# Reordering the start of a Fourier-mixing and feed-forward kernel: a weight piece behind the input, one fold by products, an earlier second stage two

## The chip, the cores and the metric

The kernel runs on one core of a Trainium2 chip. The metric is the device time of one execution in microseconds (us). Three executions of the kernel before took 1935.2, 1939.07 and 1940.8 us; the median is 1939.07. A core has five instruction streams that run side by side and wait for each other through semaphores: PE (matrix products; loads of its weights are listed as PEld), DVE (vector), ACT (activations and copies), POOL (general purpose) and SP (here only issuing transfers). Transfers are issued by SP, ACT or POOL and carried out by 16 DMA engines.

## The reference

The input x has shape (8, 3008, 256). It goes through a Fourier transform along the sequence and one along the feature axis, of which only the real part is kept. The result, as 24064 rows of 256, goes through a feed-forward layer whose activation is h * relu6(h + 3) / 6:

```python
X = np.fft.fft(x, axis=1)
X = np.fft.fft(X, axis=2)
x = X.real.astype(np.float32).reshape(B * S, D)
h = x @ w_in                      # (256, 2048)
g = h * np.clip(h + 3.0, 0.0, 6.0) / 6.0
out = (g @ w_out).astype(np.float32)   # (2048, 256)
```

The two weights arrive as 64-bit floats and are turned into 32-bit floats on the chip.

## The kernel before, in words

**Transform.** The length 3008 is split into 47 x 64. Stage one is a product with a 47-point table (`F`), stage two a product with a 64-point table (`T`). Between the stages the spectrum changes its layout through DRAM: SP and ACT store it (`zd`, line 361, later rest at line 1102), SP reads it back as `g` (line 428). The transform along the features is folded into the first weight (`fold_w_in`: PE products with the table `C`, a copy to `W1`, then SP moves one row of W1 into `WN`, line 819). The eight sequences are worked on in four pairs. The first pair is special: its first sequence (`halves[0]`) is loaded in four pieces by eight indirect transfers, two for each piece (`load_half`, line 174), so that the feed-forward can start before the second sequence is there.

**Folding x.** Each piece is added to its mirror image, first along the features (lines 215 and 216). For pieces in `FULL` a second pass builds sums and differences in a tile `y` (lines 224 to 233), and stage one needs four wide products (lines 328, 331). For the others this second pass is left out: one small add (line 219), and PE makes up for it with four times as many products, with shorter or equal rows, that read the near and the far half separately (line 344). The pieces come in the order `ORDER` = 3, 0, 1, 2. The last one (`SPLIT`) is done in two halves (lines 204, 339, 344).

**Weights.** Sixteen pieces of 512 KB come as 64-bit numbers (`load_w`, lines 727 and 731, issued by POOL). For each: ACT takes the exponent's two halves out of the top bits (`exponent_a`, line 747), PE adds them (`exponent_b`, line 761), ACT turns the sum into a power of two (`exponent_c`, line 764), DVE makes the fraction (`mantissa`, lines 772 and 773), and DVE multiplies the two (`join`, line 781 for W_in, 787 for W_out). Pieces 0 and 1 are the first of W_in, 2 and 3 the first of W_out. Pieces 4 to 9 are issued behind a small POOL copy (`see`, line 881) that waits until `g` has landed.

**Feed-forward.** A chunk is 256 columns; a step is a chunk and a group of 2 x 128 hidden features: products u and v (line 537), then s, u, v, gates on DVE (lines 546 to 586) with a relu on ACT (583), then products with the second weight into `acc` (610, 630). There are 384 steps. In the first eight (`first_steps` and `second_steps` in turn) the remaining weight pieces are made between them.

**What sets the order.** Each engine runs its instructions in the order in which the program issues them; the order is written out by hand (a manual schedule). Tiles come from pools with a fixed number of buffers; a new tile waits until the buffer's last reader is done. Two pools matter here: `ps_d`, one PSUM bank, which takes piece 1's exponent (`own=True`), every filler written without a bank of its own, and, once `starting[0]` is False, the results of stage two; and `ps_h`, three banks for u and v. `beside(p)` puts transfers and other side work at given steps (`put(t, f, ...)`). `keep_awake(n)` is filler: n products of ones with zeros, whose result nobody reads (line 831).

Of the kernel before, what the change touches and what calls it, by code (L numbers as in the profile page):

```python
# [58 lines left out]
def kernel(  # L59
# [76 lines left out]


    ORDER = [NM - 1] + list(range(NM - 1))
    FULL = (ORDER[0], ORDER[2])
    SPLIT = ORDER[NM - 1:]  # L140

    def x_tile(pool=xpool, tag="x"):
# [46 lines left out]
    def load_half(hb, m):  # L189
        start = hb.b * N1 * N2 * D  # L190
        gather(hb.x[m], NP * NXC + m, P, start + D)
        gather(hb.xr[m], m, P, start)
# [526 lines left out]
    def load_w(j):  # L719
        kind, n, i = PIECES[j]  # L720

        pool, tag, bufs = (wpool, "st", 2) if j in STRAIGHT else (spool, "t", None) if j in (2, 3) else (xpool, "x", None)
        st = pool.tile([P, 2 * WB], I32, tag=tag, bufs=bufs, name="st")
        o = st[:].bitcast(moe_w_in.dtype)
        if kind == "in":
            cs = slice(in_column(n, i), in_column(n, i) + WB // 2)
            nc.gpsimd.dma_start(out=o.rearrange("p (c j) -> p c j", c=2),
                                in_=moe_w_in[:, cs].rearrange("(c p) f -> p c f", p=P))
        else:
            r = (2 * n + i * NF) * P  # L730
            nc.gpsimd.dma_start(out=o.rearrange("p (c j) -> p c j", c=2),
                                in_=moe_w_out[r:r + 2 * P, :].rearrange("(c p) d -> p c d", p=P))
        raw[j] = st
# [6 lines left out]

    def exponent_a(j):
        top = raw[j][:].bitcast(I16).rearrange("p (n four) -> p n four", four=4)[:, :, 3]
        for i in range(2):
            low = PM[j % len(PM)][:, i].bitcast(U8).rearrange("p (n two) -> p n two", two=2)[:, :, 0]
            nc.scalar.activation(low, top, AF.Identity, bias=bias[:, i:i + 1], scale=(1 - 2 * i) / 16.0)

# [17 lines left out]
    def mantissa(j):  # L766
        st = raw[j]
        hi = st[:].rearrange("p (n two) -> p n two", two=2)[:, :, 1]
        lo = st[:].bitcast(U32).rearrange("p (n two) -> p n two", two=2)[:, :, 0]
        top = wpool.tile([P, WB], I32, tag="top", bufs=3, name="top")  # L770
        frac = top[:].bitcast(F32)
        nc.vector.tensor_scalar(top[:], hi, 0xFFFFF, 0x100000, op0=AL.bitwise_and, op1=AL.bitwise_or)
        nc.vector.scalar_tensor_tensor(frac, lo, 2.0 ** -32, top[:], op0=AL.mult, op1=AL.add)
        fracs[j] = frac
# [47 lines left out]
    def load_t(gr, ks=slice(0, 2 * KK), queue=nc.sync):  # L822
        for b in range(2):
            queue.dma_start(out=T[b * N2:(b + 1) * N2, b, gr, :, ks], in_=c_stage2[:, gr, :, ks])


    def keep_awake(n, ps=None):
        if ps is None:
            ps = ps_d.tile([P, 2 * TB], F32, tag="d", name="awake")
        for i in range(n):  # L830
            nc.tensor.matmul(ps[:], ones[:], Z[:], start=True, stop=True)  # L831
# [50 lines left out]

    for j in range(2):
        load_w(j)
    nc.gpsimd.affine_select(E[:, 0], ones[:], pattern=[[-1, P]], compare_op=AL.is_equal, fill=0.0, base=0,
                            channel_multiplier=1)
    nc.scalar.mul(E[:, 1], E[:, 0], -1.0)
    for k, m in enumerate(ORDER):  # L890
        load_half(hb, m)
    nc.gpsimd.dma_start(out=C[:], in_=c_dim.rearrange("(h p) d -> p h d", p=P))
    load_t(0, queue=nc.gpsimd)
    for j in range(2, 4):
        load_w(j)
    for j in range(2):
        exponent_a(j)
        mantissa(j)
    exponent_b(0)
    keep_awake(2)  # L900
    exponent_b(1, own=True)
    nc.scalar.copy(zero_slot(hb), first_slot[PB:PB + N1, 0:D])
    exponent_c(0)
    exponent_c(1)
    clear_table(1)
    keep_awake(2, bank([P, 2 * TB], "awake"))
    for k, m in enumerate(ORDER):
        if m in SPLIT:
            for j in range(2):
                fold_columns(hb, m, j, nc.vector)  # L910
            join(0)
        for part in range(2) if m not in SPLIT else ():
            fold_half(hb, m, part, nc.vector)
        stage1_early(hb, m)
    later[:] = later[4:6] + later[0:4] + later[6:8]
    load_g_half(hb, 0)

    seen = wpool.tile([P, 1], F32, tag="seen", name="seen")
    see(hb.g[0][:, 0, 0:1])
    for j in range(4, 10):  # L920
        load_w(j)
    take_half(halves[1], ORDER[0], cpool, "c")
    load_half(halves[1], ORDER[0])

    join(1)
    fold_w_in(0)
    fold_w_in(1)
    mantissa(2)
    exponent_a(2)
    exponent_b(2)  # L930
# [5 lines left out]
    keep_awake(2)  # L936
    join(2)

    stage2_half(hb, 0)
    spread_by_pe(hb, bank([P, TB], "ps3")[:])  # L940
    tail(3)
    starting[0] = False
    spare = [ps_a.tile([P, 2, WB // 2], F32, tag="acc", name="spare") for h in range(2)]

# [4 lines left out]
    def beside(p):  # L949
        ahead, behind = {}, {}  # L950

        def put(t, f, *a, at=ahead):
            at.setdefault(t, []).append((f, a))

        cur = pairs[p]

        if p == 0:
            for gr in range(1, NG):
                put(gr + 1, load_t, gr)
            put(1, load_g_half, halves[0], 1)  # L960
            put(5, spread_half, halves[0], 1)
            put(NF - 1, close_w)
            for i, t in enumerate((3, 5, 7, 8)):
                put(t, mix_w_out, i)
            for gr in range(2, NSG):
                put(8 * gr - 10, load_g_half, halves[0], gr)
                put(8 * gr - 5, stage2_half, halves[0], gr)
                put(8 * gr - 4, spread_half, halves[0], gr)

            hb = halves[1]  # L970
            put(1, load_zero, zero_slot(hb), hb, nc.sync)
            for k, m in enumerate(ORDER):
                if k > 0:
                    put((5, 8, 11)[k - 1], take_half, hb, m)
                    put((5, 8, 11)[k - 1], load_half, hb, m)
                for part in range(2):
                    put((4, 6, 11, 14)[k] + part, fold_half, hb, m, part, nc.gpsimd)
                put((8, 10, 15, 18)[k], stage1_quarters, hb, m, at=behind)
            for gr in range(NSG):
                put(8 * gr + 23, load_g_half, hb, gr)  # L980
                put(8 * gr + 27 - (gr == 0), stage2_half, hb, gr)
                put(8 * gr + 28 - (gr == 0), spread_half, hb, gr)

        def s2(t, pr, gr):
            for i in range(2):
                put(t + 3 + 4 * i, stage2, pr, gr, i)
            put(t + 8, spread, pr, gr)

        for gr in range(1 if p > 0 else NSG, NG):
            if gr > 1:  # L990
                put(NST * (gr - 2) + 12, load_g, cur, gr)
            s2(NST * (gr - 1), cur, gr)
        if p + 1 < NP:
            nx = pairs[p + 1]
            for c in range(NXC):
                t = 9 * c if p > 0 else 24 + 6 * c
                put(t, load_x, nx, c)
                put(t + 3, fold, nx, c, 0, nc.gpsimd)
                put(t + 5, fold, nx, c, 1, nc.gpsimd)
                put(t + 8, stage1, nx, c, at=behind)  # L1000
            put(NST * (NG - 1) - 2, load_g, nx, 0)
            put(NST * (NG - 1) + 8, load_g, nx, 1)
            s2(NST * (NG - 1), nx, 0)
        return ahead, behind
# [14 lines left out]
    uv = mlp1_products(*chunk(0))  # L1019
    activate(*chunk(0), *uv)  # L1020

    head(4)
    head(5)
    uv = mlp1_products(*chunk(1), between=lambda: keep_awake(3))

# [30 lines left out]
    def second_steps(s):  # L1058
        j = 2 * s + 4
        if j - 2 < len(PIECES):  # L1060
            if s == 1:
                see(WN[:, NF + 2:NF + 3])
            head_b(j)
            join(j)
            head_b(j + 1)
            if s == 1:
                mlp2_first(*chunk(s), halves=(0,))
                exponent_b(j + 1)
            exponent_c(j + 1)
            if j + 2 < len(PIECES):  # L1070
                head(j + 2)
            join(j + 1)
            if j + 3 < len(PIECES):
                exponent_a(j + 3)
                if s > 1:
                    head_b(j + 3)
            if s > 1:
                mlp2_first(*chunk(s), halves=(0,))
            if s == 3:
                stage2_half(halves[0], 1)  # L1080
            mlp1(*chunk(s + 1))
            if s == 1:
                head_b(j + 3)
            return
        mlp1(*chunk(s + 1))
        combine(*chunk(s + 1))
        mlp2_first(*chunk(s), halves=(0,))
        mlp1(*chunk(s + 2))
        mlp2_first(*chunk(s), halves=(1,))
# [117 lines left out]
```

## Time and profile before

| what | us |
|---|---|
| median of three executions | 1939.07 |
| the profiled execution | 1934.84 |
| its span, first to last instruction | 1933.1 |
| PE busy | 1917.7 |
| POOL busy | 1442.3 |
| DVE busy | 1426.8 |
| ACT busy | 679.5 |
| first x piece complete, DVE starts to fold | 11.68 |
| DVE starts on the last x piece | 20.02 |
| first fold of W_in on PE | 22.75 |
| read of `g` issued | 26.88 |
| first stage two on PE | 29.83 |
| first products u | 31.63 |
| stage two of group 1 on PE | 63.45 |

The table by stage gives PE's busy time for a stretch, the timeline the start and length of each instruction, and the chain of waits follows the work that ended last back from instruction to instruction. Times in the lower rows are starts, in us from the first instruction. A busy PE is not PE at its peak: fillers count as busy.

### The profile page before, as it was taken

The numbers are of one execution on the slowest core, as the hardware profiler recorded it, in microseconds if no ns is written. First come the engines' busy times: TensorE is split into PE (matmuls) and PEld (weight loads), VectorE is DVE, ScalarE is ACT, GpSimd is POOL, SyncE is SP. The second block draws the span as 40 slices with busy tenths as digits, with TensorE's granted clock in tenths as the row PEclk, the third lists the DMA queues.
The fourth block names the chain that finished last, engine by engine and source line by source line (L and its number), as shares of the span: only waits on it lengthen the run. The fifth ranks groups of instructions, "written<-read, shape, count | busy, mean of one in ns | idle before, by whom it ended". The sixth has DMA issues, their size and how long they took to land.

```text
span 1933.1 us, 28199 instructions
## 1 busy us (share of the span) xinstructions
PE 1917.7 (99%) x9360; PEld 1652.9 (86%) x9360; DVE 1426.8 (74%) x2761; ACT 679.5 (35%) x1164; POOL 1442.3 (75%) x1650
## 2 busy tenths in 40 slices
PE   9999999999999999999999999999999999999997
PEld 5688888888988888888898888888899888888887
DVE  6867776777777777777787777777778777777777
ACT  6533333333333333333333333333333333333332
POOL 4597888896688778787678787878676667666664
PEclk9999999999999999999999999999999999999999
DMA  8432232211112222121111221221110101101000
GB/s 273 129 88 50 57 86 67 63 44 39 31 36 71 57 52 55 45 56 36 27 38 50 51 55 44 54 55 46 36 28 20 28 17 29 33 12 28 21 18 20
DMA packets 154344, 98.77 MB, mean 51 GB/s; under 512 B 121877, under 2 KB 135806, under 8 KB 154198
## 3 DMA queue, kind: packets, MB, share of 16 engines
q1 hardware_dynamic: 142130, 57.45, 12.2%
q0 software_dynamic: 11360, 39.30, 7.0%
q8 instruction: 73, 1.20, 0.3%
q14 instruction: 73, 0.60, 0.1%
q10 hardware_dynamic: 708, 0.23, 0.1%
HBM read 59.61 MB, written 37.32 MB: 50 GB/s over the span
## 4 chain that ended last, share of the span: by engine, by line
PE 95%; DVE 3%; ACT 1%; DMA 0%; issue 0%; POOL 0%; DVEq 0%; ACTq 0%; POOLq 0%
PE acc L630 56%; PE v L537 16%; PE u L537 16%; PE ps L486 2%; PE ps L279 1%; PE acc L610 1%; DVE a L586 1%; DVE s L546 1%; ACT t L583 0%; DVE o L691 0%; PE spare L813 0%; DMA xt<-in_x_dram,IX 0%; PE ps L447 0%; DVE u L567 0%; PE awake L831 0%
## 5 line engine op out<-in xcount | busy, mean ns | idle before, releaser
L600 POOL TENSOR_TENSOR c<-a 128x512 f32<-128x512 f32 (+1 forms) x375 | 469.1, 1251 | 359.8 <-PE acc L630 298.1
L630 PE MATMUL acc<-c,G 128*128 128x256 f32 (+1 forms) x3008 | 697.2, 375 | 0.0
L583 ACT ACTIVATE t<-u,half 128x512 f32<-128x512 f32 (+1 forms) x384 | 260.6, 679 | 1144.1 <-DVE u L556 1064.4
L630 PEld LDWEIGHTS acc<-c,G 128*128 128x128 f32 x3008 | 565.2, 190 | 71.6 <-POOL c L600 0.4
L546 DVE SCALAR_TENSOR_TENSOR s<-qn,WN,u 128x256 f32<-128x256 f32 (+1 forms) x768 | 330.5, 472 | 338.7 <-PE u L537 338.2
L630 PE MATMUL acc<-a,G 128*128 128x256 f32 (+1 forms) x2256 | 541.6, 375 | 0.0
L630 PEld LDWEIGHTS acc<-a,G 128*128 128x128 f32 x2256 | 421.0, 189 | 73.6 <-issue 20.2
L537 PE MATMUL v<-q,W 127*128 127x256 f32 (+1 forms) x1536 | 389.3, 375 | 1.0 <-DVE a L586 1.0
L537 PE MATMUL u<-q,W 128*128 128x256 f32 (+1 forms) x1536 | 388.0, 375 | 0.2 <-ACT q L450 0.2
L586 DVE SCALAR_TENSOR_TENSOR a<-t,u 128x512 f32<-128x512 f32 (+2 forms) x448 | 264.1, 602 | 101.4 <-ACT t L583 95.6
L537 PEld LDWEIGHTS v<-q,W 127*128 127x128 f32 x1536 | 288.0, 190 | 42.1 <-DVE a L586 2.0
L537 PEld LDWEIGHTS u<-q,W 128*128 128x128 f32 x1536 | 285.8, 190 | 36.9 <-issue 1.9
L600 POOL TENSOR_TENSOR c<-a,c 128x256 f32<-128x256 f32 (+1 forms) x375 | 268.5, 716 | 29.4
L600 POOL TENSOR_TENSOR c<-c,a 128x256 f32<-128x256 f32 (+1 forms) x375 | 268.4, 716 | 29.4
L556 DVE TENSOR_TENSOR u<-s,v 128x512 f32<-128x512 f32 x352 | 245.0, 696 | 38.1 <-DVE s L546 1.8
L586 DVE SCALAR_TENSOR_TENSOR a<-t,v 128x512 f32<-128x512 f32 (+1 forms) x480 | 263.7, 566 | 0.1
L583 ACT ACTIVATE t<-v,half 128x512 f32<-128x512 f32 (+1 forms) x384 | 260.5, 679 | 0.2 <-PE acc L630 0.2
L558 DVE TENSOR_TENSOR v<-v,s 128x512 f32<-128x512 f32 x352 | 243.9, 693 | 0.0
L600 POOL TENSOR_TENSOR r<-w,e 128x256 f32<-128x256 f32 (+1 forms) x92 | 88.7, 984 | 3.6
L640 ACT ACTIVATE e<-acc 128x512 f32<-128x512 f32 (+2 forms) x184 | 83.4, 544 | 0.0
L691 DVE STREAM_TRANSPOSE o<-r 128x256 f32<-128x256 f32 (+1 forms) x192 | 72.6, 415 | 0.2
L600 POOL TENSOR_TENSOR w<-w,e 128x512 f32<-128x512 f32 (+1 forms) x46 | 57.5, 1250 | 3.6
(133 smaller groups left out, 777.0 us busy)
## 6 DMA issues: line engine op xcount, KB each, us to landing
out_dram<-o SPq DMA_DIRECT2D x747, 32.0 KB
g<-zd SPq DMA_DIRECT2D x42, 256.0 KB
zd<-z SPq DMA_DIRECT2D x48, 192.0 KB
xt<-in_x_dram POOLq DMA_DIRECT2D x21, 256.0 KB, 3.7
st<-in_moe_w_in_dram POOLq DMA_DIRECT2D x8, 512.0 KB, 6.7
st<-in_moe_w_out_dram POOLq DMA_DIRECT2D x8, 512.0 KB, 8.4
qn<-qd SPq DMA_DIRECT2D x16, 256.0 KB
xt<-in_x_dram POOLq DMA_DIRECT2D x17, 192.0 KB, 4.1
```

The lines of the kernel that those rows point to most:

```text
L279: nc.tensor.matmul(ps[b][h * PB:(h + 1) * PB, 0:n], F[rows(b), 0:PB], y[rows(b), 2 * h:2 * h + n], start=True, stop=not last, skip_group_c ...
L486: nc.tensor.matmul(ps[:, blk, u * P:n].rearrange("p (b k) -> p b k", b=2), g[:, kk, blk * (P + 1):blk * (P + 1) + P], T[:, :, gr, blk, kk, ...
L537: nc.tensor.matmul(ps[:, i, 0:nq], W1[r, blk, f * P:(f + 1) * P], q[r, blk, of:of + nq], start=True, stop=True)
L546: nc.vector.scalar_tensor_tensor(s[:, i, 0:nq], qn[:, of:of + nq], WN[:, f:f + 1], u[:, i, 0:nq], op0=AL.mult, op1=AL.add)
L556: nc.vector.tensor_tensor(u[:], s[:], v[:], op=AL.add)
L558: nc.vector.tensor_tensor(v[:], v[:], s[:], op=AL.subtract)
L583: nc.scalar.activation(t, h, AF.Relu, bias=half[:], scale=scale)
L586: nc.vector.scalar_tensor_tensor(dst, t, 1.0, h, op0=AL.min, op1=AL.mult)
L600: (eng or nc.gpsimd).tensor_tensor(out, in0, in1, op=AL.add)
L630: nc.tensor.matmul(ch.acc[i // 2][:, i % 2, 0:ch.n], G[:, i, fc, :], mv, start=(fc == 0 and i % 2 == 0), stop=(fc == NF - 1), skip_group_c ...
L640: nc.scalar.mul(ch.e[:, k:i + 1, 0:ch.n], ch.acc[i // 2][:, 0:i + 1 - k, 0:ch.n], 1.0 / WS)
L691: nc.vector.transpose(o[:, 0:n // DH, h], ch.r[:, m, h, 0:n].rearrange("p (j i) -> p j i", i=DH))
```

## The change

- `FULL` shrinks from pieces 3 and 1 to piece 3 alone. Piece 1, the third to come, is folded along the features only and goes through the short products.
- Weight piece 1 is loaded behind the eight loads of x instead of ahead of them, and then C; pieces 2 and 3 come ahead of T(0) instead of behind it. Piece 1's exponents and mantissa move behind the first stage: the first of its two exponent halves on ACT after the third piece of x (`k == NM - 2`), the rest after the loads issued behind `see`. Its join stands behind the first `fold_w_in`, followed by one filler.
- Ahead of x, two fillers, piece 1's exponent and two fillers become five fillers in one bank.
- `g` of group 1 is read right behind `g` of group 0 (before: at step 1), and `see` looks at it. T of group 1 is loaded on SP behind the second `fold_w_in` (before: at step 2). The other T loads come one step earlier, the spread of group 1's last row at step 2 instead of 5.
- `tail(3)` comes ahead of the first stage two. Stage two of group 1 moves from step 3 to between the first chunk step's activation and the second's products; between the latter's u and v there is one filler instead of three.

```diff
-    FULL = (ORDER[0], ORDER[2])
+    FULL = ORDER[:1]
...
-    def exponent_a(j):
+    def exponent_a(j, signs=range(2)):
         top = raw[j][:].bitcast(I16).rearrange("p (n four) -> p n four", four=4)[:, :, 3]
-        for i in range(2):
+        for i in signs:
...
-    for j in range(2):
-        load_w(j)
+    load_w(0)
...
         load_half(hb, m)
+    load_w(1)
     nc.gpsimd.dma_start(out=C[:], in_=c_dim.rearrange("(h p) d -> p h d", p=P))
-    load_t(0, queue=nc.gpsimd)
     for j in range(2, 4):
         load_w(j)
-    for j in range(2):
-        exponent_a(j)
-        mantissa(j)
+    load_t(0, queue=nc.gpsimd)
+    exponent_a(0)
+    mantissa(0)
     exponent_b(0)
-    keep_awake(2)
-    exponent_b(1, own=True)
     nc.scalar.copy(zero_slot(hb), first_slot[PB:PB + N1, 0:D])
     exponent_c(0)
-    exponent_c(1)
     clear_table(1)
-    keep_awake(2, bank([P, 2 * TB], "awake"))
+    keep_awake(5, bank([P, 2 * TB], "awake"))
...
         stage1_early(hb, m)
+        if k == NM - 2:
+            exponent_a(1, (0,))
     later[:] = later[4:6] + later[0:4] + later[6:8]
     load_g_half(hb, 0)
+    load_g_half(hb, 1)
...
-    see(hb.g[0][:, 0, 0:1])
+    see(hb.g[1][:, 0, 0:1])
...
+    mantissa(1)
+    exponent_a(1, (1,))
+    exponent_b(1, own=True)
+    exponent_c(1)
+    fold_w_in(0)
     join(1)
-    fold_w_in(0)
+    keep_awake(1)
     fold_w_in(1)
+    load_t(1)
     mantissa(2)
...
+    tail(3)
     stage2_half(hb, 0)
     spread_by_pe(hb, bank([P, TB], "ps3")[:])
-    tail(3)
     starting[0] = False
...
-            for gr in range(1, NG):
-                put(gr + 1, load_t, gr)
-            put(1, load_g_half, halves[0], 1)
-            put(5, spread_half, halves[0], 1)
+            for gr in range(2, NG):
+                put(gr, load_t, gr)
+            put(2, spread_half, halves[0], 1)
...
     activate(*chunk(0), *uv)
 
+    stage2_half(halves[0], 1)
     head(4)
     head(5)
-    uv = mlp1_products(*chunk(1), between=lambda: keep_awake(3))
+    uv = mlp1_products(*chunk(1), between=lambda: keep_awake(1))
...
-            if s == 3:
-                stage2_half(halves[0], 1)
```

## The prediction

> **What bounds the kernel now.** I read the page first: busy shares and chain.
>
> ```profile
> PE 1917.7 (99%) x9360; PEld 1652.9 (86%) x9360; DVE 1426.8 (74%) x2761; ACT 679.5 (35%) x1164; POOL 1442.3 (75%) x1650
> ...
> PE 95%; DVE 3%; ACT 1%; DMA 0%; issue 0%; POOL 0%; DVEq 0%; ACTq 0%; POOLq 0%
> ```
>
> PE ends the span. A table by stage has it busy 399.8 of every 400 us from 400 to 1600 us, and the edits lie ahead of 90 us. So a microsecond won or lost there on the path moves the end by as much; the main part will not change. Next, the chain of waits of the first 40 us (start, length, what):
>
> ```profile
> 5.02 6.56 DMA xt<-in_x_dram,IX
> ...
> 17.19 1.80 PE ps L344 x30
> ...
> 19.94 0.87 PE ps L328 x6
> ...
> 21.90 0.93 PE ps L344 x32
> 22.82 3.65 PE wps L813 x16
> 26.47 0.43 PE ex L761 x2
> 26.91 0.86 PE awake L831 x2
> 27.76 0.43 PE ex L761 x2
> 28.20 1.72 PE awake L831 x4
> 29.91 1.06 PE ps L447 x8
> ...
> 34.49 2.58 PE awake L831 x6
> 37.07 0.86 PE v L537 x4
> 37.93 1.72 PE acc L610 x4
> ```
>
> Input until 11.6, folds and first stage until 22.8, then the trip of the spectrum through DRAM, which PE covers with 7.09 us of weight folding and fillers until stage two at 29.91. The timeline shows that trip:
>
> ```profile
> 23.68 0.69 ACTq L361 DMA_DIRECT2D zd<-z  x1
> ...
> 26.88 0.41 SPq L428 DMA_DIRECT2D g<-zd  x1
> ...
> 29.75 0.18 POOL L881 COPY seen<-g 128x1 f32<-128x1 f32 x1 [12.90 <-DMA g<-zd]
> ...
> 30.25 1.42 POOL L727 DMA_DIRECT2D st<-in_moe_w_in_dram  x2 [0.32 <-DVE G L787]
> ```
>
> The filler ends (29.92) just when g is there (29.75). Then the DMA queues from 17.85 to 21.70 us, in which SP issued four stores of the spectrum:
>
> ```profile
> q0 software_dynamic: 322, 1.07, 103.5%
> ...
> zd<-z SPq DMA_DIRECT2D x4, 64.2 KB
> ```
>
> POOL's queue holds all engines and SP's queue moves no packet: what is issued late waits for what is queued. Last, landing of the weight loads that POOL issues at 33.1 and 33.8 us:
>
> ```profile
> DMA to landing us min/median/max: 8.8/9.2/9.5
> ```
>
> **The change, part by part.** Sums are made in the profiled execution (1934.84 us; span 1933.1, 1.74 around it); the median of the runs shown, 1939.07, is 4.23 above it, and I add the difference to the median.
>
> *Second weight piece behind x.* Pieces 0 and 1 land 6.4 and 6.8 us after issues at 1.37 and 2.28, so 1.3 apart, and the x gathers follow every 1.25 us, each 6.6 us after its issue. Taking one 512 KB load out moves x ahead by 1.2 (bounds 0, if POOL's issue sets the pace, and 1.3). DVE starts folding at 10.45 instead of 11.68.
>
> *Third x piece by products.* DVE loses two adds of 0.69 and 0.68 and a 0.17 one becomes a 0.17 one. PE swaps the 0.87 of L328 for a second 1.80 like the first L344 block: +0.93. DVE was waiting for x there (0.53 before L204), so only PE counts: first piece of products until 17.8, second until 19.7, the two split halves 0.99 and 1.04: last product at 21.75 instead of 22.83. Gain 1.1 (bounds: 0.2, if x is not earlier and all 0.93 counts; 1.9).
>
> *More fillers ahead of x.* Five at 0.86 (4 before) and no second exponent; PE ends them at about 14.15, when the first fold, over at 15.40 before, ends at 14.17. Nothing; if they run longer, 0 to 0.86.
>
> *Piece 1's work after x.* Here the order of the instructions decides. Before, both joins were done by 24.2 and PE ran 7.09 us without waiting. In the changed kernel PE's next instruction after the last product is the exponent of piece 1, and it waits for ACT: copy of z 0.59 (DVE's half 0.69), DMA issue 0.69, second exponent half 0.74: about 2.3 with the steps between. Then, in a row: ex 0.43, first fold of W_in 1.82, DVE's copy to W1 0.69, DVE's join(1) 0.68, filler 0.86, second fold 1.82, ex 0.43, filler 0.86, ex 0.43, two fillers 1.72: 9.74. The row is serial because the filler writes the one bank `d` that holds piece 1's exponent, free only after join(1), and on DVE join(1) stands behind the copy that waits for the first fold. With 0.4 for seven hand-overs (0.03 to 0.1 each in the rows) it is 12.4 against 7.09. Stage two starts at 21.75 + 12.4 = 34.1 instead of 29.91: a loss of 4.2. Its cover is gone: g, bound by the queue and issued at 26.3 to 26.9, lands ahead of that. Bounds: 2.5 (no hand-over cost, exponent half early) to 5.5. On ACT the first half waits for piece 1's landing with z's copies behind it; x's last gather and one load later, 19.3 to 20.6, against 21.0 when ACT gets there: nothing, up to 1 if late. SP now issues g(1) behind g(0), 0.5 each; the POOL copy that looks at g(1) lets the weight loads go at about 30.2, as before.
>
> *T(1) and the second stage two.* T(1) is issued on SP behind W1's second copy (31.2) and three WN loads of 0.6: 33.0 and 33.65. By then POOL has issued five weight loads since 30.2. Loads issued at those times land 8.8 to 9.5 us later, and if SP's two take their turn behind them, T(1) is there at about 42.3 (bounds: 36.5, the 2.87 of the g load without a queue; 43.3). Stage two of group 1 now stands on PE between chunk 0's products, over at 37.6 (31.63 to 33.63 before, +4.1), and the second u; everything on PE waits for it. Stall 4.7. WN's three loads wait too, but s needs the first of them only at 36.7, and it lands about 36.
>
> *Fillers three to one.* Behind the stall: stage two 1.06, u 0.86, filler 0.86, v 0.86: v ends at 45.95 instead of 37.93. The two fillers saved (1.72) and the 1.06 added are in that sum. Stage two leaves step 3 (1.06 on PE, 0.58 on ACT), but there DVE carries the chain, from 49 to 70 us: nothing (bounds 0 and -1.1). The T loads one step earlier and the row's spread at step 2 stand on SP, whose waits there are for W's copies: nothing.
>
> **Sum.** v of chunk 1 is 8.0 us late, and acc, exponents and DVE's stretch hang on it: 1934.84 + 8.0 = 1942.8 profiled, 1947.1 by the median.
>
> [...] Row: no packet of SP's queue between 17.85 and 21.70; and in 53 to 57 us POOL's queue has 70.6% of the engines and SP's 20.2%. [...]
>
> **The rivals.**
> - *T(1) isn't held up by POOL's queue.* It lands at 36.5, PE doesn't stall for it. Then the filler behind the second u waits for ACT's copy of the second stage two, behind both relus (36.11 before, 40.3 now, plus 0.58): filler until 41.75, v until 42.6: +4.7, so 1943.8. For it: the 20.2%; against: the empty stretch. [...]
> - *The clock drops in the stall.* PE rests 4.7 us. Fillers of the first 3.4 us stand 0.86 us per half apart, later ones 0.43, and the last eight microseconds of the span show a granted clock of 0.61. Up to 3.4 us at half speed: +1.7, so +9.7, 1948.8. [...]
> - *Faster: the weight chain is covered after all.* If join(1) and its exponent come early enough (piece 1 landing by 18, its halves before the last products), PE's row shrinks to 7.95 and ends at 29.7, before g; T(1) is issued before the weight loads. Then the x gain of 1.1 and 0.66 of fillers stay: -1.8, so 1937.3. It decides if the row costs under 8.2. Against: the order of DVE's and PE's instructions.
> - *Only part of T(1)'s wait counts:* W1 ready a microsecond sooner puts it behind fewer loads, at 39 to 40.5: +5.0 to +6.2, 1944 to 1945.3.
>
> **How the numbers follow.** Forecast, held up behind POOL's queue: 0.45, own range 1945.5 to 1948.5. With the clock drop: 0.17. Part of the wait: 0.10. No hold-up: 0.21. Faster or nothing: 0.07. The time is the forecast's, 1947.1. The range runs from 1941.5 (the first rival with the lower bound of the serial row) to 1952 (T at 43.3 and the clock). 0.3%, about what a measurement of this kernel can tell from no change, is 5.8 us: slower takes the first two and a third of the third, 0.65; same 0.31; faster by that much would need more than the x gain, 0.04.
>
> **What would show it.** Right: last L344 near 21.7; an idle stretch of PE before L761; W1's two copies some 4 us apart; the first L447 near 34; an idle stretch ahead of the second L447 that ends with T's landing near 42, and no packets of SP's queue while POOL's holds the engines; then the same gaps as before, 8 us late. Wrong: L447 near 30 (the row is covered), T landing by 37 (queues share), or PE faster from 70 us on, which nothing in the diff would explain.

## The result and the profile after

The changed kernel takes 1949.26 us (median of seven executions, 1944.5 to 1950.51) against 1935.07 for the kernel before beside it: 1.0054 of its time, 95% interval 1.004 to 1.0068 (taken over all executions; the two medians alone give 1.0073). The forecast was 1947.1, in a range of 1941.5 to 1952.0, and slower. Both kernels run at two levels: the one before mostly near 1935 and in about a third of its executions at 1938.9 or more, most of them near 1940.8; the change at 1944.5 to 1945.2 in three of the seven and at 1949.3 to 1950.5 in four. The profiled execution is one of 1949.26, its span 14.5 us above the one before.

The page's busy shares and the chain's shares by engine, of the kernel after:

```profile
PE 1923.4 (99%) x9384; PEld 1657.1 (85%) x9384; DVE 1425.0 (73%) x2759; ACT 680.0 (35%) x1164; POOL 1444.5 (74%) x1650
...
PE 94%; DVE 3%; POOL 1%; ACT 1%; DMA 1%; issue 0%; SPq 0%; DVEq 0%; ACTq 0%; POOLq 0%
```

Nothing changed in kind: PE ends the span. The difference lies in the start, in the chain of waits (start, length, what):

```profile
20.87 1.12 PE ps L344 x29
...
22.01 0.70 DVE z L352
...
22.78 0.69 ACTq L361
...
23.52 0.76 ACT PM L747
...
24.32 0.59 PE ex L761
24.90 3.15 PE wps L813 x8
...
28.68 0.69 DVE wi L781
...
29.41 1.12 PE awake L831 x2
30.54 1.74 PE wps L813 x8
...
32.30 0.69 DVE W L815
...
35.81 9.88 DMA T<-in_c_stage_dram
...
45.93 2.05 PE ps L447 x8
47.98 1.71 PE u L537 x4
49.69 1.71 PE awake L831 x2
51.40 0.98 PE v L537 x4
52.38 1.72 PE acc L610 x4
```

Before, the block of folds began at 22.82 and `acc` at 37.93. Now the last product is 0.84 earlier (21.99) and `acc` 14.45 later. The serial row stands there as forecast: exponent, fold, join behind DVE's copy, filler, fold. Then the chain leaves PE, in the end for a transfer of 9.88 us: T(1), issued at 34.86 and 35.81, is there at 45.7, and PE, which was done with v at 39.27, waits 6.66. Where the chain goes over to PE for good, the v products that stood at 70.30 stand at 84.73: 14.43 of the 14.45 are still there, and the span is 14.5 longer.

Most of what the forecast had too small is in the length of the same instructions. A fold of eight records takes 3.15 at 24.90 and 1.74 at 30.54; a filler 1.71 at 49.69 and 0.86 in the kernel before. The table by stage, cut at the clock changes that the trace records (columns: stretch, length, busy time and number for PE, PEld, DVE, ACT and POOL, granted clock, DMA share, GB/s):

```profile
20.79:24.20 3.41, 1.51 (x44) 1.06 (x36) 1.72 (x3) 2.21 (x6) 0.00 (x0) 1.00 1.00 330
24.20:27.62 3.42, 3.30 (x8) 2.61 (x8) 0.00 (x0) 2.75 (x6) 0.00 (x0) 0.50 0.24 58
...
37.86:41.27 3.41, 1.40 (x7) 0.89 (x5) 1.29 (x3) 0.00 (x0) 0.00 (x0) 1.00 1.03 379
41.27:44.68 3.41, 0.00 (x0) 0.00 (x0) 3.16 (x6) 1.29 (x2) 0.00 (x0) 0.50 1.05 310
44.68:48.10 3.42, 2.17 (x9) 2.20 (x10) 1.15 (x3) 0.08 (x1) 0.00 (x0) 0.50 0.27 89
48.10:51.51 3.41, 3.41 (x7) 2.02 (x7) 0.00 (x0) 3.07 (x5) 0.80 (x2) 0.50 0.00 0
```

The granted clock falls to half twice, each time behind a stretch of 3.41 us in which PE was busy for 1.4 to 1.5, and the second time it stays there until 51.51. So the first fold (all but its last 0.4 us), and all of PE's work between the stall and v, ran at half speed.

### The profile page after: what moved, and what is told of

Same layout as the page of the kernel before. It is cut to its first block, busy times and chain, and to the rows that moved or that the text cites. A ratio compares the mean times of both kernels' runs of the same rounds, so it can differ in the third digit from the quotient of the medians.

```text
span 1947.6 us, 28248 instructions
## 1 busy us (share of the span) xinstructions
PE 1923.4 (99%) x9384; PEld 1657.1 (85%) x9384; DVE 1425.0 (73%) x2759; ACT 680.0 (35%) x1164; POOL 1444.5 (74%) x1650
## 4 chain that ended last, share of the span: by engine, by line
PE 94%; DVE 3%; POOL 1%; ACT 1%; DMA 1%; issue 0%; SPq 0%; DVEq 0%; ACTq 0%; POOLq 0%
PE acc L630 55%; PE v L537 16%; PE u L537 16%; PE ps L486 2%; PE ps L279 1%; PE acc L610 1%; PE awake L831 1%; DVE a L586 1%; DMA T<-in_c_stage_dram 1%; DVE s L546 1%; ACT t L583 0%; POOL c L600 0%; PE ps L447 0%; DVE o L691 0%; DVE u L567 0%
## 5 line engine op out<-in xcount | busy, mean ns | idle before, releaser
L537 PEld LDWEIGHTS u<-q,W 128*128 128x128 f32 x1536 | 286.3, 190 | 37.5 <-issue 2.4
```

The costliest lines, as they stand in the source:

```text
L537: nc.tensor.matmul(ps[:, i, 0:nq], W1[r, blk, f * P:(f + 1) * P], q[r, blk, of:of + nq], start=True, stop=True)
```

## The experiments

The theory going in: three losses in a row on one path. The row of PE is serial (+5.6 at the first stage two), T(1) waits its turn behind weight loads that POOL issued earlier (+6.7), and PE's two rests lower its clock. Rivals: T(1) is slow by itself or the stall has another cause; the clock costs nothing because it falls beside waits; the front is a gain and only the second half loses.

**T(1) ahead of the weight loads.**

```diff
     load_g_half(hb, 1)
+    load_t(1)
...
     fold_w_in(1)
-    load_t(1)
```

> T(1) is read right behind g(1), ahead of the rows of WN and of the weight loads. Theory (T(1) waits its turn behind the weight loads that POOL issued before it): T(1) is there by 31, the second stage two starts when v of chunk 0 is done, near 39.3, no idle stretch of 6.7 us, and the second drop of the clock is gone. What is left: WN's late row (s at 39.9), so v of the second step ends near 45.5 instead of 52.4: 7 us off, a span near 1940.7. Rival (the stall is the group's g or its bank, or a transfer of SP's that is slow by itself): the second stage two stays near 45 and the span near 1947.6.

Measured: 1941.22 (median of 10, 1939.33 to 1944.63), 1.0026 of the kernel before (1.0014 to 1.0038); 8.0 below the change. The span of the profiled execution is 1938.1. Its chain:

```profile
34.21 0.91 PE ps L447 x8
...
37.02 0.87 DVE s L546 x2
...
40.49 0.48 ACT q L450
...
42.14 0.86 PE v L537 x4
43.01 1.72 PE acc L610 x4
```

No stall, and no T in the chain. v ends at 43.0, earlier than the 45.5 expected: in this execution, one of the faster ones, the clock stayed at 1.00, W1's second copy came 1.5 earlier than in the change, and s began at 37.02 where 39.9 was expected. What is left above the kernel before is the serial row and ACT's copy ahead of the filler. The rival that puts the stall on g or on the bank is out: they are unchanged here.

**The weight loads behind T(1).** The other way round: T(1) stays where the change has it, and the copy that lets the weight loads go looks at it.

```diff
-    see(hb.g[1][:, 0, 0:1])
-    for j in range(4, 10):
-        load_w(j)
...
     load_t(1)
+    see(T[:, 0, 1, 0, 0, 0:1])
+    for j in range(4, 10):
+        load_w(j)
```

(The loads of the other sequence's first piece move along.)

> Everything as in the change, T(1) too where it puts it; only the POOL copy that lets the weight loads 4 to 9 go looks at the first of T(1)'s two transfers instead of at g(1). Theory (WN's rows and T(1) take their turn behind loads that POOL issued earlier): with no load ahead of them T(1) lands about 3 us after its issue, at 36 to 38 instead of 45.7, WN's rows by 35.5, s near 37; the weight loads start some 6 us later and their pieces become the next wait, but a short one: v of the second step near 43 to 44.5, 6 to 8 us off, a span of 1939 to 1942. Rival (SP's transfers are slow by themselves at this point): T(1) still takes 9 to 10 us, and the later weight loads come on top: 1952 or more.

Measured: 1941.81 (1939.7 to 1942.78), 1.0026 (1.0017 to 1.0035). T(1)'s first transfer was issued at 36.19. The timeline of POOL:

```profile
38.96 0.19 POOL L881 COPY seen<-T 128x1 f32<-128x1 f32 x1 [21.27 <-ACT qn L470]
39.50 1.45 POOL L727 DMA_DIRECT2D st<-in_moe_w_in_dram  x2 [0.35 <-issue]
```

2.8 us from the issue of the first transfer to its use, where in the change the second took 9.9 to land, from the same queue at the same place in the program: the transfer isn't slow by itself, POOL's loads make it so. The weight loads started 9.1 us later than in the change (39.50 for 30.41) and nothing was lost by it: v of the second step ended at 45.8, 7.9 later than in the kernel before, and the span is 8.0 longer.

How the loads hold T(1) up stands in the queues of the change. WN's three rows were issued on SP just ahead of T(1), the last at 34.21, but from 33 to 36.5 us only POOL's queue (q0) moves packets. Then SP's (q1) does; these are the packets, MB and share of the 16 engines from 39.3 to 41 us and from 41 to 43:

```profile
q0 software_dynamic: 169, 0.63, 97.6%
q1 hardware_dynamic: 170, 0.00, 6.2%
...
q0 software_dynamic: 146, 0.53, 81.5%
q1 hardware_dynamic: 150, 0.12, 23.2%
```

In both stretches the two queues move about one packet for one, 169 for 170 and 146 for 150. From 36.8 to 41.3 us SP's packets are the 4-byte pieces of WN's rows, 385 of them, which stand ahead of T(1) in SP's own queue; T(1)'s packets of 2 KB follow until 45.0. They start just when POOL's six weight loads are through (3.11 of 3.15 MB by 41.3), which alone would leave open what T(1) waited for; in the next run, with fillers, they start at 37.2, with 1.47 of the 3.15 MB moved, and again right behind the rows. So T(1) does not wait for the loads to be done. In the run above, with no load of POOL's beside them, the rows' 432 packets were through between 35.4 and 37.5 and T(1) by 39.2. So the rows ahead are quick alone, 432 packets in 2.1 us, and slow beside POOL's loads, 385 in the 4.5 us in which POOL's queue moved 404 packets of 4 KB. Why SP's queue moved nothing before 36.8 stays open. How late T(1) would be beside the loads without the rows ahead of it, no run shows: with T(1) first, it was through before the loads began.

**Fillers in the two rests.**

```diff
     exponent_a(1, (1,))
+    keep_awake(2)
     exponent_b(1, own=True)
...
+    keep_awake(7)
     stage2_half(halves[0], 1)
```

> Two fillers ahead of piece 1's exponent and seven ahead of the second stage two, both in stretches in which PE was idle (2.0 and 6.7 us). Theory (the clock drops in these stretches cost time on the path): granted clock 1.00 all through, the first fold 1.8 instead of 3.15, T(1) issued 1.3 earlier and there near 43.5, second stage two, u and filler 2.8 instead of 5.5: 4 to 5 us off, a span near 1943. Rival (the drops lie beside waits and cost nothing): 1947 to 1948; more if the fillers delay PE.

Measured: 1944.62, five executions from 1944.38 to 1945.08; 1.0038 (1.0022 to 1.0053); 4.6 below the change. The chain:

```profile
21.77 1.93 PE awake L831 x4
...
24.50 1.74 PE wps L813 x8
...
37.45 6.02 PE awake L831 x14
...
43.52 1.16 PE ps L447 x8
...
45.54 0.93 PE awake L831 x2
46.48 0.86 PE v L537 x4
```

Work that nobody reads, put into time in which PE had nothing to do, makes the kernel faster, because the clock stays up: its mean is 0.998 or 0.999 in the five executions, for 0.994 to 0.997 in the change. The fold takes 1.74 again, and what follows the stall takes 3.82 instead of 6.45. The spread of 6 us between executions of the change is gone; three of its seven were about as fast as this without the fillers. The second stage two starts 2.4 earlier, but T(1) is there earlier than that: its last packet moves at 40.9, against 45.0 in the change, where it had landed 0.7 after that. So from about 41.6 on, an estimate from these figures, the fillers themselves hold PE, until 43.47: seven are some 2 us too many here.

**join(1) ahead of the first fold.**

```diff
+    join(1)
     fold_w_in(0)
-    join(1)
     keep_awake(1)
```

> join(1) ahead of the first fold of W_in, so that on DVE it no longer stands behind the copy that waits for that fold. Theory (PE's row is serial through DVE: fold, copy, join, filler, fold): PE's second fold starts near 28.9 instead of 30.5, the first stage two near 33.9, T(1) is issued 1.6 earlier and there near 43.5 to 44: about 2 us off, a span of 1945 to 1946. Rival (the row's length does not matter, because T(1) decides and lands at a time of its own): the first stage two is earlier, but the span stays at 1947 to 1948.

Measured: 1944.47, but from 1938.41 to 1946.56; 1.0029 (1.0015 to 1.0043). In the profiled execution (span 1942.7) the second fold starts at 28.90 and T(1)'s last transfer, issued at 34.05, is there at 41.7. The direction is the theory's, and the size can't be read: the clock fell twice here as well, at other moments, and that weighs as much as the edit.

**The front alone.** The second half undone: g(1), T(1), stage two of group 1 and the three fillers at their old places.

```diff
-    load_g_half(hb, 1)
-    see(hb.g[1][:, 0, 0:1])
+    see(hb.g[0][:, 0, 0:1])
...
-    load_t(1)
...
-    stage2_half(halves[0], 1)
...
-    uv = mlp1_products(*chunk(1), between=lambda: keep_awake(1))
+    uv = mlp1_products(*chunk(1), between=lambda: keep_awake(3))
```

(with the old lines for step 1, 2, 3 and 5 put back)

> The second half of the change is undone: g(1), T(1), the second stage two and the three fillers are where they were before; load order, products for the third piece, piece 1's later work and the five fillers stay. Theory (the front costs its serial row): last product near 22, first stage two near 35, v of the second step near 44 instead of 37.9: 5.5 to 6.5 us above the kernel before, a span near 1939. Rival (the front gains the earlier x and the second half is the whole loss): 1931 to 1933.

Measured: 1941.1 (1938.59 to 1943.11), 1.002 (1.0009 to 1.0032), by the medians 5.6 above the kernel before beside it. The chain has a wait that I had written off:

```profile
32.93 0.69 DVE W L815
...
33.65 7.26 DMA WN<-W
...
40.94 0.49 DVE s L546
...
44.19 1.13 PE v L537 x4
```

Without T(1) in the way, the next that the weight loads hold up is WN's row, 512 bytes that are issued once W1's second copy is done: 7.26 us, and s stands at 40.94 instead of 33.05. The front loses by itself, by the lateness of that copy, to which the clock adds: in this execution it was at half from 25.02 to 31.85.

**The second half alone**, on the kernel before, with T(1) behind g(1) and no filler in the second step:

```diff
     load_g_half(hb, 0)
+    load_g_half(hb, 1)
+    load_t(1)
...
+    stage2_half(halves[0], 1)
     head(4)
     head(5)
-    uv = mlp1_products(*chunk(1), between=lambda: keep_awake(3))
+    uv = mlp1_products(*chunk(1))
```

(the copy looks at g(1); the lines at steps 1, 2, 3 and 5 as in the change)

> The kernel before with the second half alone: g(1) and T(1) read right behind g(0), the copy looks at g(1), stage two of group 1 between the first two steps, no filler there. Theory (moving stage two of group 1 costs nothing where T(1) is there, because PE waits at this place for a bank anyway): T(1) lands by 32, v of the second step 0.5 earlier to 0.5 later than 37.1, the span within 1 us of the kernel before. Rival (the place itself is bad: ACT's copy ahead of the exponents of pieces 4 and 5, weight loads 0.5 later): 1 to 3 us above it.

Measured: 1935.11 (1934.38 to 1940.43), 0.9997 (0.9985 to 1.0009): the same. The place costs nothing where T(1) is there.

**The products alone**, on the kernel before:

```diff
-    FULL = (ORDER[0], ORDER[2])
+    FULL = ORDER[:1]
```

> The kernel before with the third piece of x by products alone. Theory (DVE waits for the last x piece anyway, PE has 0.9 more): last product 0 to 0.9 later than 22.8, the span 0 to 1 us above the kernel before. Rival (the fold was on the path): 0.5 to 1.5 us below it.

Measured: 1935.7 (1934.83 to 1941.81), 1.0005 (0.9992 to 1.0018): the same within what can be told. In the profiled execution the last product is 0.4 later (23.25) and `acc` 0.9 (38.83), which is the expected cost of PE's longer work.

**The row put in order.** All parts of the change kept; what the experiments blamed taken out.

```diff
     load_g_half(hb, 1)
+    load_t(1)
...
     mantissa(1)
+    fold_w_in(0)
     exponent_a(1, (1,))
     exponent_b(1, own=True)
     exponent_c(1)
-    fold_w_in(0)
     join(1)
-    keep_awake(1)
+    keep_awake(1, bank([P, 2 * TB], "awake"))
     fold_w_in(1)
-    load_t(1)
...
-    keep_awake(1)
...
-    keep_awake(2)
...
-    uv = mlp1_products(*chunk(1), between=lambda: keep_awake(1))
+    uv = mlp1_products(*chunk(1))
```

> The change with its row put in order: first fold of W_in ahead of piece 1's exponent, join(1) ahead of the second fold without a copy that waits in between, one filler in a bank of its own, T(1) read right behind g(1), the three fillers behind the second fold and the one in the second step left out. Theory (the loss is the serial row, and WN and T(1) behind the weight loads because of it; x is 0.8 to 1.2 earlier and g 0.6): W1's second copy near 28.7, WN's row lands by 31.5, first stage two near 29.2, s near 32.4, v of the second step near 36.5 instead of 37.1: 0 to 1.5 us below the kernel before. Rival (piece 1 behind x costs something else too, as its exponent half on ACT ahead of z's copies, or the clock): 2 us or more above it.

Measured: 1934.41, twelve executions from 1933.89 to 1935.24; 0.9986 (0.9977 to 0.9996). Its chain:

```profile
22.86 3.40 DMA zd<-z
...
26.38 2.66 DMA g<-zd
...
29.17 1.14 PE ps L447 x8
...
30.98 1.15 PE u L537 x4
...
35.86 1.13 PE v L537 x4
```

The wait for the spectrum's trip is now on the path and PE's weight work hides beside it; v starts 1.2 earlier than before. With the order of a few instructions, the place of T(1)'s two loads and four fillers fewer, the 14 us of the change are gone.

**Two more fillers ahead of x**, on the kernel before, for its two levels.

```diff
-    keep_awake(2, bank([P, 2 * TB], "awake"))
+    keep_awake(4, bank([P, 2 * TB], "awake"))
```

> The kernel before with two more fillers ahead of x, which close the stretch from 13.9 to 15.4 us in which PE has little to do. The kernel before has run at two levels in these comparisons, most executions near 1935 and about a third near 1940.8; the repaired row with five fillers there ran at one. Theory (at some phases of the clock's window this stretch lowers the clock, which costs those executions some 5 us): the upper level goes, all executions near 1935. Rival (the upper level is from elsewhere, as the last filler or the gap behind the stores): it stays in about a third of them.

Measured: 1934.98, eleven executions from 1934.78 to 1935.58, none at the upper level; the kernel before beside it from 1934.37 to 1940.96, 0.9996 (0.9987 to 1.0005). The lower level is not faster, the upper one is gone; beside it the kernel before was there in two of 15, and in the repetition below in six of 21 against none of eleven.

**The repaired row beside it**, both once more on one chip:

> The repaired row once more, beside the kernel before with two more fillers on the same chip. Theory (the repaired row has a gain of its own, v of the second step at 35.9 instead of 37.1): all executions within 1 us of each other, 0.5 to 1.2 below the other's. Rival (its gain is only that it runs at one level): the two are the same within 0.3.

> The kernel before with two more fillers ahead of x, as the other side of that comparison. Theory: all executions near 1935, 0.5 to 1.2 above the repaired row. Rival: the two are the same within 0.3.

Measured: 1934.32 (1933.89 to 1935.6) against 1934.97 (1934.76 to 1935.39), eleven executions each; against the kernel before 0.9993 (0.9984 to 1.0002) and 0.999 (0.998 to 1.0). Nine of the eleven repaired ones lie below the lowest of the other, two at its top (1935.38 and 1935.6 beside 1935.39): a gain of 0.65 us by the medians, of the size expected, in a total that few measurements would show. The two ratios don't show it: their intervals overlap, and they stand in the other order. The greater part of the 0.9986 above came from the missing upper level, as the medians there are only 0.88 apart.

## Why the prediction was right, and where it was short

- *Direction and places* held: slower, by a serial row and by T(1), late because of POOL's loads. The sum, 8.0 us, was too small for the profiled 14.45 and for the ratio's 10 (0.0054 of 1935). That 1947.1 lies so near 1949.26 is in part luck: 4.23 of it came from the three executions shown, two of which were at the upper level. Beside the change the kernel before had a median of 1935.07, and 8.0 more is 1943.1.
- *Second piece behind x:* DVE started to fold at 10.60 (10.45 forecast), the last product at 21.99 (21.75). A gain of 0.84 instead of 1.1. Right.
- *Third piece by products:* nothing clear of noise by its own experiment, and 0.9 at `acc` in its profiled execution, where 0.93 of PE's time was counted. Right.
- *The serial row:* 34.1 forecast, 35.54 measured for the first stage two in the timeline. Of the 1.4, 1.33 is the first fold at half clock. With the clock up (T(1) first) it is 34.21. The row was right, the clock was missing from it: I had weighed the clock only for the later stall.
- *T(1):* there at 45.69 instead of 42.3, past the bound of 43.3. It was issued 2.2 later (1.3 of it the slow fold) and took 9.9 where I took 8.65, which is below the 8.8 to 9.5 of its own row. This term was mis-sized. That it hangs on POOL's loads was shown from both sides; that it takes its turn behind them, with no packet of SP's queue until they are done, was wrong. It moved while they did, behind 385 small packets of WN's rows. A time read from the landing of POOL's own loads came near to that, but it was not the mechanism.
- *WN's row lands about 36, and s needs it at 36.7:* wrong. The second of the two s waited for it until 39.95, hidden behind the longer stall; with the second half undone it was the stall.
- *Behind the stall* 3.64 forecast, 6.45 measured: half clock. That was the second rival, at 1.7 us and 0.17; it came, together with the forecast's own case, and cost 2.81 here and 1.33 in the first fold, by which T(1) was issued later. The rival was under-priced and should not have been one: a forecast with two rests of PE has to carry the clock in its main sum.
- *More fillers ahead of x: nothing.* So it is for the lower level; for the upper one it was wrong, as two more fillers alone show.
- *T(1) isn't held up by POOL's queue* (the first rival): SP's queue did move beside POOL's from 36.8 us on, 170 of its packets against 169 of POOL's from 39.3 to 41 us. The rival's time was wrong all the same. Its 36.5 left out that SP's queue moved nothing from 33 to 36.5, and that WN's rows went ahead of T(1), 385 packets until 41.3.
- *Faster after all:* the condition named, a row under 8.2, is what the repaired kernel meets; it gained 0.65 by the medians, not 1.8, as g and not the row then holds PE until 29.17.

## What to carry to other kernels

Look at what a transfer shares the engines with: T(1) took 9.9 us beside POOL's loads and 2.8 without them. When an edit moves a small load past a release of large ones, count the pieces that stand ahead of it in its own queue, since here 385 pieces of 4 bytes took 4.5 us beside 404 packets of 4 KB of the other, and ask which other small transfers slip behind the same release. A reordering on one engine has to be read as rows across engines: one copy that waits for PE, ahead of the join that PE waits for, turned two parallel strands into one. And PE's rest ahead of the second stage two cost twice, once as the wait, 6.66 us, and once as half speed on what followed, 6.45 us for work that took 3.82 with fillers in the rest. Fillers should end before the wait does: the seven here held PE some 2 us longer, by the estimate above.

## What was not expected of the hardware

The trace's records change the clock in steps of 3.41 us, and it falls without a whole step of rest: half clock came behind stretches in which PE was busy for 1.51 and 1.40 of them. In the execution with T(1) ahead of the loads a stretch with 1.96 did not lower it; in the front alone, one with 1.34 did, and one with 2.03 did not raise it again:

```profile
22.99:26.40 3.41, 1.96 (x9) 1.47 (x8) 0.86 (x2) 2.30 (x4) 0.00 (x0) 1.00 0.68 177
26.40:29.81 3.41, 2.03 (x8) 1.31 (x8) 1.28 (x2) 1.63 (x3) 0.00 (x0) 1.00 0.53 175
```

```profile
21.61:25.02 3.41, 1.34 (x6) 0.90 (x5) 1.72 (x3) 1.98 (x4) 0.00 (x0) 1.00 0.95 305
25.02:28.43 3.41, 2.03 (x6) 1.12 (x4) 1.28 (x2) 2.51 (x4) 0.00 (x0) 0.50 0.22 49
28.43:31.85 3.42, 3.42 (x6) 2.06 (x7) 0.00 (x0) 0.00 (x0) 2.15 (x4) 0.50 0.37 73
```

(The first pair is the execution with T(1) first, the second the front alone.) So in these rows 1.51 of 3.41 us and less came ahead of half clock, and 1.96 did not; what lies between, no row shows. Behind the 2.17 after the stall of the change the clock stayed at half, behind the 3.30 of the first fold it was back at 1.00. The steps start at another moment in each of three profiled executions (the first recorded change is at 5.09 us in the kernel before, 7.14 in the change and 5.92 with T(1) first), which would let the same rest lower the clock in some and not in others. This fits the spread of the change, whose three faster executions have a mean granted clock of 0.997 and the four others 0.994 or 0.995, and the constant time once the rests are filled, with 0.998 or 0.999. That the start of the steps decides is argued, not shown.

With two more fillers ahead of x the kernel before has no upper level in 22 executions. That level is one of the clock: of the 97 executions of that kernel beside the experiments, the 31 at 1938.9 or more all have a mean granted clock of 0.995 or 0.996, and the 66 others 0.998 or 0.999. Where in them the clock falls no trace shows, since the profile of that kernel is of the lower level. There the least busy 3.41 us ahead of 23 us has PE busy for 2.15, more than in the rows above behind which the clock fell. That stays open.
